# RetNet recurrence and SwiGLU block on one core: the half-head loads cut by token half, and the plan in another order

## The chip, the core and the metric

The kernel runs on one core of a Trainium2 chip. A core has a matrix engine (TensorE, PE in the profile, with its weight loads as PEld), a vector engine (VectorE, DVE), an activation engine (ScalarE, ACT), a general engine (GpSimd, POOL) and SyncE (SP), which here only waits and issues DMAs. Sixteen DMA engines carry the transfers. The metric is the device time of one execution in microseconds; runs of one kernel are given by their median.

## The reference

Two blocks follow one another. The first is a retention layer over q, k, v of shape (batch 4, heads 8, tokens 768, width 64):

```python
state = gamma[None, :, None, None] * state + np.einsum('bhd,bhe->bhde', k[:, :, t], v[:, :, t])
y[:, :, t] = scale * np.einsum('bhd,bhde->bhe', q[:, :, t], state)
```

with one decay gamma per head and scale 1/8. Its output, as 3072 tokens of 512 columns, is x for the second:

```python
g = x @ w_gate                      # 512 -> 1536
silu = g * (1.0 / (1.0 + np.exp(-g)))
val = x @ w_val
return (silu * val @ w_out).astype(np.float32)    # 1536 -> 512
```

## The kernel before, in words

**Segments.** The 3072 tokens are four batches of six chunks of 128 tokens. A segment is three chunks of each of two batches, 768 tokens; there are four segments, 0 to 3. Each has an up stage (gate and value products, SiLU, product of both into `hT`) and a down stage (`hT` times `w_out`). The retention of segment s+1 runs during the end of the up stage and in the down stage of segment s, between its matmuls.

**Words.** Matmuls run on float32r operands; each float32 operand is split into three words (lines 993 to 1010: a first word on ScalarE, a second on VectorE, a third on POOL or VectorE), and a product of K = 128 is three matmuls. The list `ELSE` names the steps that go to the other of two engines than usual: for third words VectorE in place of POOL.

**Segment 0** converts and splits all weights and keeps them in HBM: 12 up units `wup` (896 KB each) and 12 down units, split, `wdnt` (768 KB each). From segment 1 on, units come back by `load_unit` (`L`, line 1063) and `w_load` (`W`, line 1139). The up products of segments 1 to 3 use a seven-product scheme (`product`, line 1091): step `p f.n` is 6 matmuls of 128x384. A down step `D f.tok` (line 1160) is 3 matmuls of 128x512.

**Retention of segments 1 to 3.** A segment has three pairs p of chunks, one chunk from each batch. For a pair there are five loads `l`, issued by `load_pair`, n = 5p + w: w = 0 and 1 are k and q turned (head width on the partitions, line 789, 512 KB each in one DMA); w = 2, 3 and 4 are v, k and a second copy of q (line 793, 512 KB each in four DMAs of 128 KB, from `v_n`, `k_n`, `q_t`). These last three, the half-head loads, land as follows: of chunk c, partition 64 g + t and column 512 c + 256 z + n hold row 64 z + t, column 256 g + n of the source. So the partitions' lower and upper half hold the two halves of the 512 columns (g), and the two halves of the 128 rows (z; for v and k a row is a token) lie beside one another. The buffers (`homes`) are shared between pairs, so a load waits until what was in its home has been read.

The steps of a pair: `sc` (scores, line 798 by `scores_of`), `dec` (mask and decay), `q` (second q times decay, line 824 by 414, VectorE), `k` (k times decay, line 831, ScalarE), then `A` and `B` (`mix2`: scores times v, old state times q, and the growth of the state by k and v), `was`, `new`, `mv` (state), `y` (bank to `chunk_x`, line 1025), `sum` and `x` (the words of the next up stage's operand).

**Order.** All steps stand in one string, `PLAN`, 2345 names long; `run` calls them in that order, and each call appends its instructions to its engine's queue. Every engine works through its own queue in order; waits between engines are put in by the framework from what each instruction reads and writes. So the place of a name in `PLAN` sets its place in each queue that it touches. For SyncE that holds for `l`, `L`, `W`, `Z` (stores of split weights), `U` (raw weights) and `o` (stores of output tiles, line 1197): a DMA that waits for a buffer holds up all that stand behind it in the string.

Of the kernel before, what the change touches and what calls it, by code (L numbers as in the profile page):

```python
# [70 lines left out]
    G5:0 j4:0 n6:1 a8 G5:1 n6:3 U14:3 n5:5 W5:1 c7 i5:0 c14 i5:1
    Z13 U9:1 T5:1 j5:1 a14 U15:0 C7 W5:0 n7:0 T5:2 k5 n6:2 G6:0
    n6:4 n6:5 T6:0 T6:1 Z5 G6:1 g4 i6:0 n7:3 n7:1 n7:2 G7:0 T6:2
    j5:0 n7:4 W6:1 i6:1 n7:5 b14 b8 S14 C14 Z6 1/l1 R0 a9
    W6:0 S8 c8 C8 n8:0 n8:1 n8:2 b9 i7:0 h2 G7:1 j6:0 W7:0
    j6:1 S9 T7:0 n8:3 c15 c9 W7:1 Z14 a15 U10:2 U11:1 T7:1 C9
    n8:4 i7:1 j7:1 n8:5 b15 S15 T8:0 T7:2 U16:3 n9:0 G8:0 i8:0 G8:1
    n9:3 W8:1 T8:1 j7:0 n9:1 n9:2 T8:2 g5 a10 b10 S10 G9:0 k4
    i8:1 c10 Z7 a11 t4 C15 n9:4 C10 n9:5 W8:0 j8:1 T9:0 c16
    n10:0 b11 T9:1 Z15 G9:1 n10:3 a16 h1 n10:1 j8:0 n10:2 t5 b16  # L80
    1/l3 1/l0 S11 W9:1 W9:0 n10:4 S16 n10:5 i9:1 G10:1 c11 T10:0 C16
    C11 j9:1 i9:0 n11:0 1/cv0 Z8 U17:2 n11:1 j9:0 1/sc0 1/cv2 Z16 G10:0
    i10:1 1/cv3 0/h0.0 n11:2 1/l4 1/dec0.0 n11:3 1/k0.2 0/h0.1 W10:1 n11:4 n11:5 1/l7
    1/k0.0 i10:0 W10:0 1/l2 1/cv1 1/cm T11:0 1/dec0.1 1/q0.0 T11:1 T11:2 Z11 G11:0
    G11:1 a17 b17 0/h1.0 1/k0.1 1/k0.3 0/W0 0/W1 j10:1 S17 c17 C17 0/h0.2
    1/q0.1 1/was0.01 0/h1.1 j10:0 W11:0 i11:0 i11:1 1/l5 1/l6 0/d0.0 0/d0.1 j11:0 0/h1.2
    Z17 0/h2.0 0/h4.0 0/d1.0 1/was0.00 0/d0.2 W11:1 0/W2 0/d1.1 j11:1 T10:1 0/Z0 1/A0
    0/D0.0 0/d1.2 0/h2.1 0/D0.1 0/D0.2 1/sc1 1/l8 1/new0.0 0/h2.2 0/Z1 1/y0.00 0/d2.0 0/d2.1
    1/mv0.0 1/dec1.1 1/dec1.0 1/was0.11 0/D0.3 0/D1.0 0/D0.4 0/D0.5 0/h3.0 1/l9 0/d2.2 0/Z2 1/k1.3
    T9:2 T10:2 0/h4.1 0/D1.2 0/D1.3 0/D1.5 0/D1.1 0/h4.2 1/was0.10 1/y0.01 0/D1.4 1/k1.2 1/q1.0  # L90
    0/h5.0 0/W3 0/d3.0 0/d3.1 1/k1.1 0/h3.1 1/q1.1 1/B0 0/D2.0 0/D2.1 0/D2.2 Z10 Z9
    0/W4 1/begin 1/new0.1 0/d3.2 0/h5.1 0/h3.2 1/y0.10 1/y0.11 1/k1.0 1/mv0.1 0/D2.5 1/A1 0/D3.0
    1/x0.1.0 1/was1.00 1/x0.1.2 1/sum0.0 1/sum0.1 1/l10 0/Z3 0/D2.3 0/D2.4 0/W5 0/D3.4 0/D3.5 0/D3.1
    0/D3.2 0/d4.0 0/d4.1 1/was1.01 1/sum0.3 1/sum0.2 0/h6.0 1/l11 1/x0.2.0 1/x0.1.1 1/x0.0.0 1/x0.2.2 1/x0.2.1
    1/new1.0 1/l12 1/was1.10 1/y1.01 1/y1.00 0/d4.2 0/D4.0 0/h5.2 0/Z4 1/was1.11 1/x0.0.1 0/h6.1 0/d5.0
    0/h6.2 0/D3.3 0/D4.1 0/D4.3 0/W6 1/mv1.0 0/d5.1 1/B1 0/D4.5 0/D4.2 1/y1.11 0/d5.2 1/x0.0.2
    1/l13 0/D5.1 0/d6.0 0/d6.1 0/Z5 1/new1.1 1/y1.10 0/D4.4 0/h7.0 0/h8.0 1/sum1.0 0/D5.3 0/D5.0
    0/d6.2 0/D5.4 0/D5.5 0/D5.2 0/W7 0/h7.1 1/L0 1/k2.3 1/x1.1.0 1/mv1.1 1/k2.1 1/k2.0 0/h8.1
    0/h8.2 0/h7.2 0/Z6 0/W8 1/sc2 1/l14 0/d7.0 0/d7.1 1/x1.1.2 1/dec2.0 1/dec2.1 1/x1.2.0 0/h9.0
    1/was2.00 1/was2.01 0/D6.2 0/D6.5 0/D6.4 0/D6.3 0/D6.0 0/D6.1 1/L1 1/sum1.1 0/d7.2 0/W9 0/Z7  # L100
    1/sum1.3 1/x1.2.2 1/sum1.2 0/D7.5 1/x1.1.1 0/h9.1 0/d8.0 0/h10.0 0/d8.1 1/k2.2 0/D7.3 0/D7.0 0/D7.1
    0/D7.2 0/D7.4 1/x1.0.0 1/q2.0 1/q2.1 0/d8.2 0/Z8 0/h9.2 1/A2 0/D8.0 0/d9.0 0/h11.0 0/D8.1
    1/y2.00 0/d9.1 0/D8.3 0/D8.4 0/D8.5 0/D8.2 1/x1.0.2 1/x1.2.1 1/y2.01 0/d9.2 0/D9.0 0/h10.1 0/h10.2
    1/x1.0.1 0/W10 0/d10.0 0/d10.1 0/W11 1/w0.0.0 0/Z9 1/new2.0 1/mv2.0 0/D9.3 0/D9.2 1/B2 0/D9.1
    0/h11.1 0/d10.2 0/Z10 1/w0.0.1 1/L2 1/y2.10 1/y2.11 0/d11.0 0/D10.0 1/x2.2.0 0/D10.2 0/D10.1 1/sum2.0
    1/sum2.2 1/sum2.1 0/D9.5 0/D9.4 1/w0.1.0 1/w0.2.0 1/x2.1.0 0/d11.1 0/d11.2 0/D10.3 1/sum2.3 0/Z11 0/h11.2
    1/x2.0.0 0/D10.4 1/w0.0.2 1/x2.1.2 1/x2.1.1 0/D11.3 0/D11.1 0/D11.2 0/D11.0 0/e2 0/e0 1/x2.0.2 0/D10.5
    1/w1.2.0 0/D11.4 1/x2.0.1 1/w1.0.0 0/D11.5 1/w1.1.0 0/o2 1/x2.2.2 1/p0.0 1/w0.1.1 1/w0.1.2 1/p0.1 1/x2.2.1
    0/e1 1/u0.0 1/p0.2 1/w2.1.0 1/w1.0.1 1/p0.3 1/u0.3 1/u0.1 1/w1.0.2 1/p0.4 1/w2.2.0 0/o0 0/e4
    0/o4 0/o1 1/w0.2.1 1/L3 1/w0.2.2 1/p1.1 1/p1.0 1/w1.1.1 1/u0.4 1/u0.2 1/p0.5 1/w2.0.0 1/u0.5  # L110
    1/u0.6 1/p0.6 1/u1.0 1/p1.2 1/w2.0.1 1/w1.1.2 1/u0.8 1/w1.2.1 1/p1.3 1/w2.0.2 1/u1.3 1/p1.4 1/L4
    1/u1.1 1/u0.9 1/p2.0 1/w3.2.0 1/w3.1.0 1/w2.1.1 1/u1.4 1/w1.2.2 1/w3.1.1 1/u1.5 1/w2.1.2 1/u2.0 1/p1.5
    1/w3.0.0 1/u1.6 1/p2.1 1/u2.1 1/w2.2.1 1/p1.6 1/u1.8 1/w4.2.0 1/w3.1.2 1/u1.9 1/p2.2 1/L5 1/w3.0.1
    1/p2.3 1/u2.3 1/p2.4 1/w2.2.2 1/u2.4 0/e3 1/w3.2.1 1/w3.0.2 1/p2.5 1/u1.2 0/o3 1/u2.5 1/p2.6
# [12 lines left out]
    1/p8.1 1/u8.1 1/w10.2.0 1/w9.2.2 1/w9.1.2 2/l0 1/u7.9 1/w10.2.1 1/p8.2 1/u8.3 1/p8.3 1/p8.4 1/u8.4
    1/p8.5 1/w10.1.0 1/w10.0.0 1/u8.5 1/w9.0.2 1/u8.2 1/w10.1.1 2/l1 1/w10.1.2 1/p8.6 1/w10.0.1 1/u8.6 1/w10.0.2
    1/u7.7 1/p9.0 1/u8.8 1/w11.2.0 1/u9.0 1/p9.1 1/u9.1 1/p9.2 1/p9.3 1/u9.3 1/p9.4 1/u9.4 1/p9.5
    1/w11.1.0 2/sc0 2/l4 2/l2 1/u8.7 1/w11.0.0 1/u9.2 1/u9.5 1/p9.6 1/u8.9 1/w11.2.1 1/w11.1.1 1/w11.1.2  # L130
    1/u9.6 1/p10.0 1/u9.8 1/p10.1 1/w11.0.1 2/l5 1/W0 1/u10.0 1/p10.2 1/u10.3 2/dec0.1 1/u9.9 2/l6
    1/p10.3 1/u10.1 1/u10.2 2/dec0.0 1/p10.4 2/q0.0 1/u9.7 1/u10.4 1/p10.5 1/h0.0 1/u10.6 1/h1.0 1/u10.5
    1/h0.1 1/w11.0.2 1/w10.2.2 1/p11.0 1/p11.1 1/u11.0 1/p11.2 1/u11.1 1/u11.2 1/u10.7 1/h1.1 1/h0.2 1/p10.6
    1/u11.3 1/p11.3 1/u10.8 1/W1 1/u10.9 1/p11.4 1/h1.2 1/u11.4 1/p11.5 1/h2.0 1/h4.0 1/u11.5 2/l8
    2/q0.1 1/w11.2.2 1/p11.6 1/u11.8 2/begin 1/u11.6 1/u11.7 1/D0.0 1/W2 1/h2.1 1/D0.3 1/D0.1 1/u11.9
    2/k1.1 1/h4.1 2/A0 2/new0.0 2/sc1 2/l9 2/l7 2/y0.00 1/h4.2 1/h2.2 1/D0.2 2/mv0.0 2/dec1.0
    2/dec1.1 1/D1.2 1/D1.0 1/D0.4 1/D0.5 1/D1.5 1/W3 2/l10 1/D1.4 2/k1.0 2/was0.11 1/h3.0 2/was0.10
    2/q1.0 2/k1.3 2/y0.01 1/D1.3 1/D1.1 1/W4 1/h5.0 2/k1.2 1/h3.1 1/h5.1 2/q1.1 1/D2.0 1/D2.1
    2/B0 1/h5.2 1/D2.3 1/D2.5 1/D2.2 2/new0.1 2/y0.11 2/mv0.1 1/D2.4 1/W5 2/y0.10 2/l12 2/was1.01
# [244 lines left out]
def tile_retnet_swiglu(  # L384
# [394 lines left out]
    def two_of(t):  # L779
        return t.rearrange("p (z n) -> p z n", z=2)  # L780
# [551 lines left out]
```

## Time and profile before

| | |
|---|---|
| median of 3 runs | 668.71 us (659.56, 668.71, 670.72) |
| profiled execution | 666.25 us, its span 664.1 us |
| mean granted TensorE clock | 0.987 |
| busy: PE / PEld / DVE / ACT / POOL | 642.2 / 589.1 / 495.2 / 391.7 / 183.8 us |
| DMA | 144.59 MB, mean 218 GB/s over the span |
| DMA issues of line 793 (half-head loads) | 108, 128 KB each |
| DMA issues of line 1139 (split down weights) | 39 |

The span runs from the first to the last instruction of the profiled execution. The page divides it into 40 equal slices of 16.6 us and gives for each the busy share of an engine in tenths, the granted clock of TensorE, the mean busy share of the 16 DMA engines, and what they moved. In time: segment 0's attention and up stage run to 138 us, its down stage to 208; the up stages of segments 1 to 3 start at 208, 366 and 524, and their down stages at 303, 454 and 608. The half-head loads of segment 1 are issued from 110 to 180 us, those of segment 2 at 228 and from 287 to 340, those of segment 3 at 374 and from 438 to 493.

A line of a view of one source line gives engine, operation, tiles, count, and the duration of one in ns (least, median, greatest); for an instruction of SyncE that is the time of the issue, not of the transfer. "DMA to landing" is from issue to the last of its landing marks. A line of the view of waits gives who waited for whom, the total in us, how many times and the longest.

### The profile page before, as it was taken

The numbers are of one execution on the slowest core, as the hardware profiler recorded it, in microseconds if no ns is written. First come the engines' busy times: TensorE is split into PE (matmuls) and PEld (weight loads), VectorE is DVE, ScalarE is ACT, GpSimd is POOL, SyncE is SP. The second block draws the span as 40 slices with busy tenths as digits, with TensorE's granted clock in tenths as the row PEclk, the third lists the DMA queues.
The fourth block names the chain that finished last, engine by engine and source line by source line (L and its number), as shares of the span: only waits on it lengthen the run. The fifth ranks groups of instructions, "written<-read, shape, count | busy, mean of one in ns | idle before, by whom it ended". The sixth has DMA issues, their size and how long they took to land.

```text
span 664.1 us, 14143 instructions
## 1 busy us (share of the span) xinstructions
PE 642.2 (97%) x5587; PEld 589.1 (89%) x5587; DVE 495.2 (75%) x760; ACT 391.7 (59%) x815; POOL 183.8 (28%) x122
## 2 busy tenths in 40 slices
PE   8999999998989989999999999999889999999997
PEld 7999989886869979998878999999678899999886
DVE  3988687867989947787689778787678788777541
ACT  3778788966655656556667665546474465554221
POOL 1442545420112745520000514520000524452000
PEclk9999999997999979999999999999899999999999
DMA  9899987897986651456884724446976643403564
GB/s 314 275 353 302 373 275 256 301 321 305 319 282 217 226 157 57 154 192 210 281 308 170 255 77 167 143 147 199 287 230 229 212 153 128 167 0 100 199 220 148
DMA packets 60850, 144.59 MB, mean 218 GB/s; under 512 B 5872, under 2 KB 33008, under 8 KB 60784
## 3 DMA queue, kind: packets, MB, share of 16 engines
q1 hardware_dynamic: 60208, 142.90, 63.3%
q8 instruction: 44, 0.72, 0.4%
q10 hardware_dynamic: 576, 0.79, 0.4%
q14 instruction: 22, 0.18, 0.1%
HBM read 113.78 MB, written 29.88 MB: 216 GB/s over the span
## 4 chain that ended last, share of the span: by engine, by line
PE 58%; DMA 4%; ACT 1%; SPq 0%; issue 0%; DVE 0%; ACTq 0%
PE bank L1091 35%; PE bank L1160 19%; DMA oitem<-wdnt 3%; PE bank L798 3%; DMA loads<-in_k_n_dram 0%; SPq L793 0%; ACT loads L831 0%; ACT states L889 0%; ACT gitem L994 0%; DVE chunk_x L1183 0%; ACT tmp L1106 0%; ACT bank L1107 0%; ACT chunk_x L1185 0%; ACT bank L1110 0%; ACT xb L1003 0%
## 5 line engine op out<-in xcount | busy, mean ns | idle before, releaser
L1160 PE MATMUL bank<-oitem,gitem 128*128 128x512 f32 x867 | 209.0, 398 | 6.2 <-DMA oitem<-wdnt 4.6
L1160 PEld LDWEIGHTS bank<-oitem,gitem 128*128 128x128 f32 x867 | 163.0, 191 | 43.0 <-DMA oitem<-wdnt 2.4
L1091 PE MATMUL bank<-xa,gitem 128*128 128x384 f32 x864 | 159.9, 339 | 3.3 <-ACT tmp L1106 3.3
L1091 PEld LDWEIGHTS bank<-xa,gitem 128*128 128x128 f32 x864 | 152.9, 191 | 4.0 <-ACT tmp L1106 3.6
L1000 POOL TENSOR_TENSOR gitem<-gitem 128x768 fp32r<-128x768 f32 x48 | 96.3, 2016 | 175.1 <-DVE gitem L997 154.0
L1000 POOL TENSOR_TENSOR oitem<-oitem 128x256 fp32r<-128x256 f32 (+1 forms) x51 | 56.1, 1103 | 167.8 <-DVE oitem L997 149.8
L922 PE MATMUL bank<-xa,oitem 128*128 128x384 f32 x480 | 85.3, 336 | 2.1 <-DVE hT L459 1.1
L922 PEld LDWEIGHTS bank<-xa,oitem 128*128 128x128 f32 x480 | 82.9, 188 | 3.6 <-DVE hT L459 1.8
L997 DVE SCALAR_TENSOR_TENSOR gitem<-gitem,loads 128x768 fp32r<-128x768 f32 x72 | 75.9, 1069 | 11.4 <-ACT gitem L994 11.3
L1091 PE MATMUL bank<-xb,gitem 128*128 128x384 f32 x432 | 81.8, 335 | 0.0
L994 ACT ACTIVATE gitem<-loads 128x768 fp32r<-128x768 f32 x72 | 58.8, 841 | 34.8 <-PE bank L1091 26.2
L1091 PEld LDWEIGHTS bank<-xb,gitem 128*128 128x128 f32 x432 | 75.8, 188 | 0.2
L414 DVE SCALAR_TENSOR_TENSOR gitem<-gitem 128x768 fp32r<-128x768 f32 x72 | 71.2, 994 | 1.9
L997 DVE SCALAR_TENSOR_TENSOR gitem<-gitem,hT 128x768 fp32r<-128x768 f32 x48 | 46.0, 962 | 23.3 <-ACT gitem L994 23.2
L994 ACT ACTIVATE gitem<-hT 128x768 fp32r<-128x768 f32 x48 | 39.9, 840 | 36.8 <-PE bank L1160 29.6
L1091 PE MATMUL bank<-xb,oitem 128*128 128x384 f32 x216 | 43.8, 337 | 0.0
L1108 DVE TENSOR_TENSOR hT<-bank,tmp 128x384 f32<-128x384 f32 x36 | 20.0, 555 | 30.6 <-PE bank L1091 29.9
L1107 ACT COPY tmp<-bank 128x384 f32<-128x384 f32 x36 | 17.2, 477 | 36.0 <-PE bank L1091 20.1
L1091 PEld LDWEIGHTS bank<-xb,oitem 128*128 128x128 f32 x216 | 38.0, 188 | 0.2
L889 ACT ACTIVATE states<-states,local 128x64 f32<-128x64 f32 x120 | 31.5, 335 | 1.5 <-DVE states L897 1.5
L1025 ACT COPY chunk_x<-bank 128x256 f32<-128x256 f32 x36 | 12.4, 367 | 30.4 <-DVE states L897 16.1
L1108 ACT COPY tmp<-bank 128x384 f32<-128x384 f32 x36 | 17.3, 480 | 14.1 <-PE bank L1091 14.0
(125 smaller groups left out, 786.2 us busy)
## 6 DMA issues: line engine op xcount, KB each, us to landing
loads<-wup SPq DMA_DIRECT2D x36, 896.0 KB, 5.0
oitem<-wdnt SPq DMA_DIRECT2D x33, 768.0 KB, 5.2
wdnt<-oitem SPq DMA_DIRECT2D x12, 768.0 KB, 5.3
wup<-first SPq DMA_DIRECT2D x9, 896.0 KB, 6.4
rawp<-in_w_gate_dram SPq DMA_DIRECT2D x12, 512.0 KB, 7.4
rawp<-in_w_val_dram SPq DMA_DIRECT2D x12, 512.0 KB, 6.5
rawp<-in_w_out_dram SPq DMA_DIRECT2D x12, 512.0 KB, 7.1
out_dram<-chunk_x SPq DMA_DIRECT2D x21, 256.0 KB, 2.3
```

What stands on the lines that cost most here:

```text
L414: stt(o, x, 1.0, y, op0=mul, op1=op)
L798: nc.tensor.matmul(o, a, b, start=start, stop=True, skip_group_check=True)
L889: act(states[:, z, g, n], states[:, 1 - z, g, n], AF.Copy, scale=lg[:, ds(NP * g + n, 1)])
L922: nc.tensor.matmul(o, w[:, a, ts(b, P)], X0[:, a, i, NC - 1 - b], start=a == b == 0, stop=a == 2 and b == NC - 1, skip_group_check=True)
L994: act(o[0], x, AF.Copy, scale=CUT / FAR)
L997: stt(o[1], f32(o[0]), -FAR, x, op0=mul, op1=add)
L1000: op(o[2], f32(o[0]), f32(o[1]), op=add)
L1025: copy(cx[:, ds(2 * r, 2), :, half[z]], y)
L1091: nc.tensor.matmul(o, w[:, a, k], x[:, a, KH - 1 - k], start=start and a == k == 0, stop=a == 2 and k == KH - 1, skip_group_check=True)
L1107: lambda: act(gate, c11, AF.Silu, scale=ONE), lambda: copy(u2, x),
L1108: lambda: copy(p5, wb), lambda: tt(h1, x, p5, op=add),
L1160: nc.tensor.matmul(banks[tok][:, cols], hs[f][:, a, ds(i * TH + u * P, P)], wo[f][:, a, cols], start=f == a == 0, stop=f == NF - 1 and a = ...
```

## The change

Two things are changed; all else is as it was.

**The half-head loads.** The four DMAs of a load were made per chunk c and per half g of the partitions: each wrote 64 partitions, two pieces of 256 columns in each, from all 128 rows and one half of the columns. Now they are made per chunk c and per half z of the rows: each writes all 128 partitions, one piece of 256 columns in each, from 64 rows and both halves of the columns. Every element lands where it did. A DMA still moves 128 pieces of 1 KB, and there are as many DMAs.

```diff
         for c in range(2):
-            for g in range(2):
+            for z in range(2):
                 nc.sync.dma_start(
-                    out=two_of(t[half[g], ts(c, 512)]),
-                    in_=src[c, :, ts(g, 256)].rearrange("(z t) n -> t z n", z=2))
+                    out=t[:, ds(512 * c + 256 * z, 256)],
+                    in_=src[c, half[z]].rearrange("t (g n) -> g t n", g=2))
```

**The order.** The first 150 names of `PLAN` stay; the 2195 behind them are the same names in another order. Half of all names move by at most 5 places, one in four by 11 or more, one in a hundred by more than 24. The farthest: the stores `0/o5`, `0/o4` and `2/o4` go 114, 221 and 247 places back, `2/l7` 63 forward, `3/l7` 38 back. Some rows that hold the loads:

```diff
-    1/l3 1/l0 S11 W9:1 W9:0 n10:4 S16 n10:5 i9:1 G10:1 c11 T10:0 C16
+    1/cv3 h1 i9:0 1/l3 j9:1 n11:0 n11:1 j9:0 n11:2 1/l2 U17:2 Z8 1/l4
...
-    1/w11.1.0 2/sc0 2/l4 2/l2 1/u8.7 1/w11.0.0 1/u9.2 1/u9.5 1/p9.6 1/u8.9 1/w11.2.1 1/w11.1.1 1/w11.1.2
+    1/w11.1.0 1/u8.7 1/u9.2 1/u9.5 1/p9.6 1/u9.8 1/w11.0.0 2/sc0 2/l4 2/l2 1/u8.9 1/p10.0 1/w11.2.1
+    1/w11.1.1 1/w11.1.2 1/p10.1 1/u9.6 1/u9.7 1/u9.9 1/w11.0.1 2/dec0.1 2/l7 2/l5 1/W0 1/u10.0 1/u10.1
...
-    2/k1.1 1/h4.1 2/A0 2/new0.0 2/sc1 2/l9 2/l7 2/y0.00 1/h4.2 1/h2.2 1/D0.2 2/mv0.0 2/dec1.0
```

The order of SyncE's steps around the loads of segment 2, before and after:

```
before  2/sc0 l4 l2 l5 W0 l6 W1 l8 W2 A0 sc1 l9 l7 W3 l10 W4 B0 W5 l12 l11 A1 W6 B1 l13 W7 sc2 W8 l14 A2 W9
after   2/sc0 l4 l2 l7 l5 W0 l6 W1 l8 W2 sc1 A0 l9 W3 l10 W4 B0 l12 W5 l11 A1 W6 B1 l13 W7 W8 sc2 l14 A2 W9
```

The list `ELSE` loses 16 names and gains 18, third words of weights nearly all:

```diff
-    "0/d1.1", "0/d11.1", "0/d4.1", "0/d5.1", "0/d8.1", "0/d9.1", "0/e3",
+    "0/d0.1", "0/d1.1", "0/d11.1", "0/d3.1", "0/d4.1", "0/d5.1", "0/d8.1",
...
```

More of the change, by code (lines that the diff above doesn't have):

```diff
@@ L71 @@
[L71 to L78, printed above, removed]
@@ L97 @@
[L97 to L102, printed above, removed]
@@ L229 @@
[L229 to L231 removed]
+    U4:3 c3 Z0 n2:1 v0:2 Z1 n2:3 y1:1 p1:2 U13:1 a4 n2:2 v1:2
+    U5:2 S12 C12 y0:2 C3 G2:1 u1:2 n2:4 n3:0 n3:1 n3:2 n2:5 b4
+    Z12 G2:0 n3:3 h0 S4 y1:2 c4 i2:0 W2:0 G3:0 W2:1 n3:4 C4
+    T3:0 U6:3 a5 n4:0 i2:1 n3:5 j2:0 W3:0 G3:1 c13 T2:0 T3:1 T3:2
@@ new lines @@
+    n8:2 G8:0 W7:0 c15 S9 c9 C9 n8:3 Z14 1/l1 U10:2 U11:1 U16:3
+    T7:1 j7:0 n8:4 i7:1 a15 n8:5 i8:0 b15 T7:2 W7:1 j7:1 T8:0 S15
+    T8:1 g5 n9:0 T8:2 n9:1 G8:1 W8:1 n9:2 n9:3 i8:1 a10 j8:1 W8:0
+    b10 S10 c10 j8:0 C10 n10:0 n10:1 G9:0 Z7 a11 b11 c16 C15
+    n9:4 T9:0 n9:5 t4 G9:1 1/l0 Z15 t5 W9:1 W9:0 n10:3 n10:4 n10:5
+    n10:2 T9:1 S11 a16 b16 S16 i9:1 G10:1 c11 T10:0 C16 C11 1/sc0
+    1/cv3 h1 i9:0 1/l3 j9:1 n11:0 n11:1 j9:0 n11:2 1/l2 U17:2 Z8 1/l4
+    i10:1 Z16 1/dec0.0 1/cv2 0/h0.0 1/cv0 G10:0 n11:3 n11:4 T11:0 T11:1 T11:2 Z11
@@ new lines @@
+    1/mv1.0 0/d5.0 0/d5.1 0/d5.2 1/x0.0.2 0/h6.2 0/D4.1 0/W6 1/B1 1/y1.11 1/l13 0/d6.0 1/was1.11
+    0/d6.1 0/Z5 1/new1.1 1/y1.10 0/D4.5 0/D4.2 1/sum1.0 0/D5.3 0/D4.4 0/h7.0 1/mv1.1 0/h8.0 0/D5.0
+    0/D5.4 0/d6.2 0/D5.2 0/D5.5 0/D5.1 0/D6.5 0/D6.4 1/sc2 0/W7 0/h7.1 1/L0 1/k2.3 1/x1.1.0
+    1/k2.0 1/k2.1 1/x1.2.0 0/h8.1 0/h7.2 1/x1.1.2 0/h8.2 0/Z6 0/W8 1/l14 0/d7.0 1/dec2.0 1/dec2.1
+    1/was2.00 0/h9.0 1/was2.01 0/d8.0 1/k2.2 0/D6.1 0/D6.2 0/D6.3 1/sum1.1 1/sum1.3 0/d7.1 0/d7.2 0/D6.0
+    0/D7.0 1/L1 0/W9 0/Z7 1/sum1.2 1/x1.2.2 0/D7.2 0/D7.1 0/h9.1 0/h10.0 0/d8.1 0/D7.3 0/D7.5
@@ new lines @@
+    2/x0.0.0 2/x0.0.2 1/h6.2 1/D4.0 1/D3.1 2/x0.0.1 2/y1.01 1/W6 1/D4.3 2/B1 2/y1.10 2/y1.11 2/x1.1.0
+    2/sum1.0 2/sum1.1 1/D4.5 1/D5.5 1/D5.2 1/D4.4 1/D4.1 1/D5.1 2/l13 2/sum1.2 2/was1.11 2/new1.1 2/mv1.1
+    2/L0 1/D5.3 1/D5.4 1/D5.0 1/W7 1/W8 1/D6.0 1/D6.3 2/sc2 1/D6.2 2/k2.3 2/was2.01 1/h7.0
+    1/h8.0 2/sum1.3 2/x1.1.2 2/x1.1.1 1/h7.1 1/h7.2 2/dec2.1 1/D6.1 2/l14 2/k2.1 2/k2.2 2/k2.0 2/dec2.0
+    1/h8.1 1/D6.5 1/D6.4 2/L1 1/h8.2 1/h9.0 2/x1.2.0 2/x1.2.1 2/q2.0 2/x1.2.2 2/q2.1 1/D7.1 1/D7.2
@@ new lines @@
+    2/u8.0 2/p8.2 2/u8.3 2/p8.3 2/u8.4 2/u7.7 2/u8.1 2/u8.2 2/p8.4 2/w10.2.1 2/u8.5 2/p8.5 2/u8.6
+    2/w10.1.0 2/w10.1.1 2/w10.1.2 3/l1 2/w9.2.2 2/p9.0 2/u9.0 2/p8.6 2/w11.2.0 2/u8.8 2/w11.2.1 2/w11.2.2 2/u8.9
+    2/p9.2 2/p9.1 2/u9.1 2/u9.3 2/p9.3 2/u9.4 2/w10.0.0 2/p9.4 2/p9.5 2/w11.1.0 2/w10.0.1 2/w10.0.2 2/w10.2.2
+    3/sc0 3/l4 2/u9.5 3/dec0.1 2/u9.2 2/p9.6 3/dec0.0 2/u9.6 2/u9.8 2/u9.9 2/u9.7 2/w11.0.0 2/w11.0.1
+    2/w11.0.2 3/l6 2/p10.0 2/p10.1 2/W0 3/l2 2/u8.7 2/u10.0 2/p10.2 2/u10.3 2/p10.3 2/w11.1.1 2/w11.1.2
@@ new lines @@
+    2/D4.3 2/D4.2 3/mv1.0 3/was1.11 3/was1.10 3/B1 3/l13 3/new1.1 3/y1.10 2/D4.4 2/D4.5 2/W7 2/h7.0
+    3/y1.11 2/h8.0 3/x1.2.0 3/x0.0.2 3/sum1.0 3/sum1.1 3/L0 2/D5.4 3/was2.01 3/k2.3 2/h7.1 3/x1.2.1 3/x1.2.2
+    3/sum1.3 2/D5.2 2/D5.5 2/D5.1 3/sc2 3/l14 3/k2.0 3/was2.00 3/mv1.1 3/k2.1 3/k2.2 2/h8.1 2/h7.2
+    2/h8.2 3/sum1.2 2/D6.5 3/dec2.1 3/dec2.0 2/D6.2 2/D5.3 2/D5.0 2/h9.0 2/h9.1 2/W8 2/D6.1 2/D7.1
+    2/D6.4 3/x1.1.0 3/L1 3/x1.0.0 3/x1.1.2 2/D6.0 2/D7.0 2/D6.3 2/D7.2 2/h10.0 3/q2.0 3/x1.1.1 3/q2.1
```

298 lines of the change are left out of this document (140 added, 158 removed).

## The prediction

> **What bounds the kernel now.** The page first: who is busy, and at what clock.
>
> ```profile
> PE 642.2 (97%) x5587; PEld 589.1 (89%) x5587; DVE 495.2 (75%) x760; ACT 391.7 (59%) x815; POOL 183.8 (28%) x122
> ...
> PEclk9999999997999979999999999999899999999999
> DMA  9899987897986651456884724446976643403564
> ...
> q1 hardware_dynamic: 60208, 142.90, 63.3%
> ```
>
> TensorE works 97% of 664.1 us, at full clock but for three short dips, so the matmuls set the time and an order of steps can win at most the 22 us in which TensorE rests and the dips. The last line is the one that the rest hangs on: of the 16 DMA engines' time 63.3% is taken, and in the first third of the span the row of tenths stands at 8 and 9.
>
> Next the waits of TensorE, and the views of the two lines that issue the attention loads and the down weights:
>
> ```profile
> PE bank L1160 <- DMA oitem<-wdnt: 4.6, 3, 2.0
> PE bank L1091 <- ACT tmp L1106: 3.3, 1, 3.3
> ```
>
> ```profile
> L793 SPq DMA_DIRECT2D loads<-in_q_t_dram x36: 595/600/1494, 120.5 to 492.5; - x36
> ...
> DMA to landing us min/median/max: 2.5/3.5/8.6
> ```
>
> ```profile
> L1139 SPq DMA_DIRECT2D oitem<-wdnt x39: 319/320/1467, 293.1 to 648.4; - x39
> ```
>
> The longest total wait is for a down weight, 4.6 us in three places. SyncE's one queue carries those weights and the 108 half-head loads of L793, each 600 ns to issue against 320 for a weight.
>
> Last, the three stretches in which the half-head loads run, by windows (length, busy time of each engine, clock, DMA share, GB/s):
>
> ```profile
> 110.00:185.00 75.00, 71.41 (x868) 61.23 (x867) 58.74 (x95) 54.62 (x135) 18.09 (x12) 0.95 0.89 300
> ...
> 287.00:345.00 58.00, 56.80 (x714) 48.85 (x711) 43.55 (x68) 36.79 (x95) 3.68 (x3) 1.00 0.77 258
> ...
> 438.00:500.00 62.00, 58.05 (x758) 49.90 (x751) 43.90 (x71) 37.57 (x94) 4.55 (x3) 0.97 0.75 230
> ```
>
> TensorE has no room there, and the DMA engines have little: 11%, 23% and 25%.
>
> **The loads, step by step.** Before, one issue moves 128 pieces of 1 KB: destination 64 partitions with two pieces each, source 64 rows with two pieces each; the outermost count is 64 on both sides. After, it moves the same 128 pieces to the same places, but the destination is 128 partitions with one piece each, and the source is written (g, t, n): two column halves outermost, 64 rows inside each. What decides is over how many DMA engines this is dealt. In the trace each of the 343 issues has 16 landing marks (5488 in all), so all 16 engines took part each time; but every one has 64 or 128 outermost on both sides. So the trace bounds the new form from both ends only: 16 engines, if the 128 destination rows are dealt out, two, if the two outermost source pieces are. No transfer in the trace shows a cut along an inner dimension, and the nearest rows differ in just this point; I take two.
>
> The Trainium skill, page "DMA: Bandwidth & Descriptors", section "Why a DMA increments its semaphore by 16 and not by 1", says that the number of engines is the largest up to 16 that divides the outermost dimension (over one) of both access patterns, and that on the queue of SyncE they are the lowest-numbered ones. The 16 marks of each issue agree with it for 64 and 128; no run here shows it for two. By it the sum is the one below; by another row of that page ("Rules for kernel authors": one 128-partition transfer rather than two of disjoint partition halves) it would be the first rival.
>
> Price of a piece: 63.3% x 16 x 664.1 us / 60208 packets is 0.112 us for a mean 2373 bytes, so 48 ns for 1 KB. With 16 engines an issue is 8 pieces on each, 0.39 us, and a load (four issues) 1.54 us. With two it is 64 pieces on each, 3.08 us, and a load 12.34 us, and if the two are the same each time, all loads queue there. Down weights, up weights and k/q loads are cut over all 16, so each has a share on those two, in order of issue behind the half-head loads: a weight is there only when its slowest share is. That puts the price on the path: first the down steps (L1160), then the attention products, wait.
>
> Now each stretch, as work of one of the two engines (share x length, less the loads at the old price, plus the loads at the new, less the stretch):
> - 110 to 185, 9 loads: 66.8 - 13.9 + 111.1 = 164.0, over by 89 us.
> - 287 to 345, 8 loads (the ninth, `2/l3`, went alone at 228): 44.7 - 12.3 + 98.7 = 131.1, over by 73.
> - 438 to 500, 8 loads: 46.5 - 12.3 + 98.7 = 132.9, over by 71.
>
> That is 233 us. It is high, since the share holds packets stretched by the crowd: the trace's 1 KB packets have a median of 46 ns and the 6 and 7 KB ones 234 and 272, and at these the same sums give 75 + 63 + 57 = 195. With two engines at work and 14 mostly waiting the crowd is gone, so I take a value nearer to the low end, 205. The two loads left out of the stretches (228 and 374) fall into up stages at shares of 0.41 and 0.46 and cost nothing; in a busy stretch each would cost its 10.8.
>
> Can the new order hide it? It moves the loads little: `2/l7` comes before the first down weight and `3/l7` behind the second; `1/l3` comes behind `1/sc0`. The queue order of SyncE is else nearly the old one: W0 stands behind two or three loads, and `l13` still waits for B1, `l14` for the second-pair scores. Nothing starts an up stage earlier.
>
> **The rest of the change.** SyncE's issue: from 600 ns to between 320 (a weight's one-piece rows) and 600 (the same split source), 0 to 30 us of 664 on a queue with gaps; beside two engines that are late it is worth nothing, alone it is in the first rival. The new order moves steps by 5 places in the median and by 24 at the 99th percentile; instructions, durations and matmuls are the same. Stores `0/o4`, `0/o5` and `2/o4` go 100 to 250 places later; a store is 256 KB, 0.7 us of each DMA engine, and frees SyncE from a wait (L1197 on L1191 was 22.0 us in six); nobody asks for their buffer in the up stage. The list ELSE loses 16 steps and gains 18: mostly third words of weights that go from POOL (1.10 or 2.02 us) to VectorE (0.53 to 1.0) and back, behind TensorE's queue on engines at 28% and 75%. Order and list together are worth between +22 (all rest of TensorE gone) and a loss of the same size; I take 0, as the old waits are short and spread, and in the stretches they lie inside the long ones. Half clock after a wait: the dips read 0.95 over 75 us, so some 4 us; between two late loads it is hidden, after the last load of a stretch it costs up to about 4 us each.
>
> Sum: the profiled execution took 666.25 us (span 664.1 and 2.1 around it), and 666 + 205 gives 871; I say 870. The runs shown have a median of 668.71, 0.4% above it, and reach from 659.56 to 670.72: 2% is about what a measurement of this kernel can tell from no change.
>
> **The rivals.**
> 1. All 16 engines carry the new form (the 128 destination rows are dealt out). Then a load stays at 1.54 us, and the gain is the shorter issue where a weight stands behind L793: three weight waits of 4.6 us, half of a dip of 3.4 us, and the 1.2 us before a state decay at 339: 7.5 us at most, 659 us. The order can add or take some 10 to either side: 650 to 677, not slower. For it: the destination is the shape of the weight loads. Against: the source is not. It decides as soon as the landing of a load stays at 3 to 4 us.
> 2. Two engines, but others at each issue. Then there is no shared queue, and each load lands 3.08 - 0.39 = 2.7 us later. Nine groups of attention products (three in each of three stages) wait that long at most: 24 us, so 666 to 690, and 678 where half of it is hidden. Against: nothing in the trace shows a choice that changes.
> 3. Two engines with their queue, but the quiet stretches before take part of it: 185 to 228 has a share of 0.65, 228 to 287 of 0.41, 345 to 438 of 0.46, so 15, 35 and 50 us are free. Were loads issued that early, 100 us would go: 770. Against: the buffers are freed by the stage itself. It is the low end of the forecast's range, as 666 + 233 + 31 = 930 is the high one (three times 4 us of half clock, and 19 us in which the two engines stand still because SyncE waits for a buffer).
>
> **Chances.** Forecast (two fixed engines) 0.84, rival 1 0.11, rival 2 0.05. Its own range of 770 to 940 holds nearly all of the first, so 0.81 altogether, and the range stops there. Slower by over 2% (above 682): 0.84 and 0.02 of rival 2, 0.86. Within 2%: 0.09 of rival 1 and 0.03 of rival 2, 0.12. Faster: 0.02.
>
> **What would show it.** The view of L793: a median of over 8 us from issue to landing, where it was 3.5; under 4 if rival 1 holds, about 6 with rival 2. TensorE's waits: L1160 behind oitem<-wdnt and L798 behind loads, tens of us each, in place of 4.6. The row of DMA tenths: about 4 in the three stretches (66.8 us of work in some 155), which grow to some 155, 125 and 120 us, while the up stages keep their length. The landing marks: two late ones, 14 at once, in each L793 issue. The prediction is wrong if TensorE's busy share stays above 95%, and too high if packets of 1 KB go faster than 46 ns on a queue of their own.

## The result, and the profile after

| | before | after |
|---|---|---|
| median (runs) | 667.75 us (5: 659.21 to 670.72) | 879.24 us (5: 875.26 to 881.18) |
| ratio | | 1.324, 95% interval 1.312 to 1.335 |
| profiled span | 664.1 us | 877.6 us |
| mean granted TensorE clock | 0.987 | 0.883 |
| issues of L793: SyncE's time in them | 71 us | 257 us |

The kernel is 32% slower. The page of after, in the parts that the prediction read of before (busy time; tenths of the clock and of the DMA engines in 40 slices, now of 21.9 us each; the queue's packets, MB and share of 16 engines):

```profile
PE 686.5 (78%) x5587; PEld 620.0 (71%) x5587; DVE 503.5 (57%) x768; ACT 390.8 (45%) x812; POOL 179.0 (20%) x117
...
PEclk9999995777769989976788898998677879999999
DMA  9899824445546443215445452523234446441454
...
q1 hardware_dynamic: 58696, 142.90, 48.1%
```

The same matmuls and the same bytes; TensorE goes from 97% of the span to 78%, and the DMA engines from 63.3% to 48.1%. The queue has 1512 packets fewer than before, 14 for each of the 108 issues of L793: the landing marks of 14 engines, which no longer carry a piece.

TensorE's waits in after (who waited for whom, us in total, times, longest):

```profile
PE bank L1160 <- DMA oitem<-wdnt: 57.2, 8, 22.9
PE bank L798 <- ACT chunk_x L1025: 28.2, 5, 18.4
PE bank L798 <- DVE loads L414: 23.5, 6, 6.5
PE bank L922 <- DVE hT L459: 23.1, 1, 23.1
PE bank L798 <- DMA loads<-in_k_t_dram: 15.4, 2, 9.9
PE bank L1091 <- ACT tmp L1106: 14.2, 2, 8.0
```

The first was 4.6 us before; the next three were 1.9, 0.6 and 1.1. The waits behind L414 hang on half-head loads, and so do the 23.1 us behind L459, ahead of which VectorE had stood 23.6 us for a second q. The longest one behind L1025 came after ScalarE had waited 11.7 us for a raw down weight. In the view of L793 (issues with least, median and greatest ns of an issue; then who waited for what they bring) the loads are what VectorE and ScalarE wait for.

```profile
L793 SPq DMA_DIRECT2D loads<-in_q_t_dram x36: 512/2536/5384, 130.2 to 700.7; - x36
L793 SPq DMA_DIRECT2D loads<-in_v_n_dram x24: 534/2632/4721, 115.0 to 620.2; - x24
...
  DVE loads L414: 90.1, 13
  ACT tmp L831: 72.0, 6
  ACT loads L831: 32.7, 6
```

The median of all 108 issues is 2.6 us where it was 0.6. A piece of SyncE's timeline of after (start, length, engine, line) shows two loads, eight issues, in 21.68 us, with a k load and a down weight behind them:

```profile
363.57 5.43 SPq L793 DMA_DIRECT2D loads<-in_q_t_dram  x4
369.04 21.68 SPq L793 DMA_DIRECT2D loads<-in_v_n_dram  x8
390.82 2.46 SPq L789 DMA_DIRECT2D loads<-in_k_t_dram  x1
393.38 0.99 SPq L1139 DMA_DIRECT2D oitem<-wdnt  x1
```

And windows of after: that piece first, then the three stretches with half-head loads (length, busy time of PE, PEld, DVE, ACT, POOL, clock, DMA share, GB/s):

```profile
363.50:390.00 26.50, 15.47 (x96) 14.44 (x87) 15.21 (x23) 7.97 (x15) 4.52 (x4) 0.90 0.13 45
...
109.00:262.00 153.00, 87.34 (x976) 72.97 (x973) 67.96 (x104) 60.20 (x142) 17.78 (x11) 0.77 0.46 161
...
363.00:479.00 116.00, 70.84 (x794) 58.04 (x784) 41.76 (x67) 36.57 (x95) 5.02 (x4) 0.79 0.37 123
...
589.00:707.00 118.00, 73.22 (x841) 61.09 (x833) 46.69 (x76) 37.42 (x95) 2.53 (x2) 0.78 0.36 115
```

A DMA share of 0.13 is two engines of sixteen, and while they work alone 45 GB/s move. The stretches grew from 75, 58 and 62 us to 153, 116 and 118; from the start of the last up stage to the end it is 140 us in both kernels. The trace's DMA records name no engine, but they show how many packets are under way; counted for each tenth of a us, with two packets read as two engines at work:

```
stretch of after   length   two packets on way    none on way
109 to 262          153           81.9 us             1.2 us
363 to 479          116           73.8                1.3
589 to 707          118           72.0                4.9
```

So for 228 us two engines worked and fourteen stood by. That they are the same two each time is seen in transfers that are cut over all 16: their marks come in two lots, fourteen early and two some 4 us late. Of the 68 such transfers that were issued in the three stretches, 64 have two marks over 1 us behind the fourteen. Three examples (ns after the issue; the last row is a half-head load's issue, whose fourteen idle marks come at once and whose two real ones late).

```
390.82 L789   fourteen 5648 to 6028    two 9899, 10521
393.38 L1139  fourteen 5479 to 5811    two 9219, 9836
369.04 L793   (14 at once) 2958        two 10210, 10756
```

Between 369.5 and 388 us 871 half-head pieces of 1 KB went, which is one in 42.5 ns on either engine. An issue is 64 of them, 2.72 us, which is about what SyncE's issues take: with some four issues (10.5 us of work) outstanding, SyncE stood in the next one until the engines had done one more.

### The profile page after: what moved, and what is told of

Its sections match the earlier page's. It is cut to its first block, busy times and chain, and to the rows that moved or that the text cites. A ratio compares the mean times of both kernels' runs of the same rounds, so it can differ in the third digit from the quotient of the medians.

```text
span 877.6 us, 14120 instructions
## 1 busy us (share of the span) xinstructions
PE 686.5 (78%) x5587; PEld 620.0 (71%) x5587; DVE 503.5 (57%) x768; ACT 390.8 (45%) x812; POOL 179.0 (20%) x117
## 3 DMA queue, kind: packets, MB, share of 16 engines
q1 hardware_dynamic: 58696, 142.90, 48.1%
## 5 line engine op out<-in xcount | busy, mean ns | idle before, releaser
L1160 PE MATMUL bank<-oitem,gitem 128*128 128x512 f32 x867 | 232.8, 427 | 69.6 <-DMA oitem<-wdnt 57.2
L1160 PEld LDWEIGHTS bank<-oitem,gitem 128*128 128x128 f32 x867 | 176.7, 208 | 115.9 <-DMA oitem<-wdnt 54.5
L1091 PE MATMUL bank<-xa,gitem 128*128 128x384 f32 x864 | 162.4, 343 | 15.6 <-ACT tmp L1106 14.2
L1091 PEld LDWEIGHTS bank<-xa,gitem 128*128 128x128 f32 x864 | 155.7, 194 | 16.9 <-ACT tmp L1106 15.0
L922 PE MATMUL bank<-xa,oitem 128*128 128x384 f32 x480 | 88.0, 343 | 23.9 <-DVE hT L459 23.1
L1000 POOL TENSOR_TENSOR oitem<-oitem 128x512 fp32r<-128x512 f32 (+1 forms) x47 | 55.3, 1180 | 236.6 <-DVE oitem L997 210.4
L922 PEld LDWEIGHTS bank<-xa,oitem 128*128 128x128 f32 x480 | 85.6, 193 | 25.4 <-DVE hT L459 23.4
L994 ACT ACTIVATE gitem<-loads 128x768 fp32r<-128x768 f32 x72 | 59.1, 842 | 27.0 <-PE bank L1091 21.9
L414 DVE SCALAR_TENSOR_TENSOR gitem<-gitem 128x768 fp32r<-128x768 f32 x72 | 69.7, 974 | 1.4 <-DVE gitem L997 0.5
L414 DVE SCALAR_TENSOR_TENSOR loads<-loads,tab 128x512 f32<-128x512 f32 x18 | 12.4, 689 | 90.1 <-DMA loads<-in_q_t_dram 83.9
L831 ACT ACTIVATE tmp<-tmp,local 128x128 f32<-128x128 f32 x24 | 8.5, 394 | 72.0 <-DMA tmp<-in_k_n_dram 72.0
L1025 ACT COPY chunk_x<-bank 128x256 f32<-128x256 f32 x36 | 12.2, 366 | 57.5 <-PE bank L798 35.1
L1107 ACT COPY tmp<-bank 128x384 f32<-128x384 f32 x36 | 17.2, 478 | 40.5 <-PE bank L1091 19.6
```

The lines of the kernel that those rows point to most:

```text
L414: stt(o, x, 1.0, y, op0=mul, op1=op)
L922: nc.tensor.matmul(o, w[:, a, ts(b, P)], X0[:, a, i, NC - 1 - b], start=a == b == 0, stop=a == 2 and b == NC - 1, skip_group_check=True)
L994: act(o[0], x, AF.Copy, scale=CUT / FAR)
L1000: op(o[2], f32(o[0]), f32(o[1]), op=add)
L1025: copy(cx[:, ds(2 * r, 2), :, half[z]], y)
L1091: nc.tensor.matmul(o, w[:, a, k], x[:, a, KH - 1 - k], start=start and a == k == 0, stop=a == 2 and k == KH - 1, skip_group_check=True)
```

## The experiments

Two figures serve all of them. The **extra work** of a load in the form after is 64 x 4 x 42.5 ns = 10.88 us on each of two engines less the 1.54 us that it was, 9.34 us. The **spare time** of an engine in the three stretches before is 8 + 13 + 16 = 37 us (11%, 23% and 25%), which the prediction subtracted. It belongs to the kernel that one compares with: in the one with 128 source rows below, whose stretches are 71.5, 57 and 58.5 us at DMA shares of 0.93, 0.82 and 0.78, it is 28 us.

**Loads alone, order alone.** Theory: the loads are the whole loss. Rival: the order has a part in it, as it puts down weights behind two or three loads. The first kernel has the order before and the loads after, the second the loads before and the order after (edits against after).

```diff
 loads alone: PLAN and ELSE of before
-    U4:3 c3 Z0 n2:1 v0:2 Z1 n2:3 y1:1 p1:2 U13:1 a4 n2:2 v1:2
+    U4:3 c3 Z0 n2:1 v0:2 Z1 n2:3 U13:1 a4 p1:2 y1:1 n2:2 S12
...
 order alone: the loads of before
-                    out=t[:, ds(512 * c + 256 * z, 256)],
-                    in_=src[c, half[z]].rearrange("t (g n) -> g t n", g=2))
+                    out=two_of(t[half[g], ts(c, 512)]),
+                    in_=src[c, :, ts(g, 256)].rearrange("(z t) n -> t z n", z=2))
```

> The old order with the new half-head loads. If the two outermost pieces of the source put each load on two engines (theory), the whole loss is here: 860 to 900 us, each issue of line 793 with 3 landing marks in place of 16, 2.6 us from issue to issue where they follow one another. If the new order were the cause (rival), this would stay at 660 to 680 us.

> The new order with the old half-head loads. Theory: the order is worth little, 650 to 680 us, 16 marks for every issue. Rival (the order brings the loss): 850 us or more.

Measured beside 662.98 us of before: loads alone 880.04 us, ratio 1.330 (1.324 to 1.336), order alone 656.16 us, ratio 0.990 (0.986 to 0.995). The loads are the whole loss; the order alone is a gain of 1.0%, invisible behind them (879 and 880 us with either order). TensorE's waits for transfers in the kernel with the order alone:

```profile
PE bank L798 <- DMA loads<-in_k_t_dram: 3.2, 1, 3.2
PE bank L1160 <- DMA oitem<-wdnt: 1.8, 4, 0.6
```

The 4.6 us for down weights of before are 1.8.

**One piece per row, eight issues.** If the source's outermost count of two is the cause, issues of 64 rows with one piece each are carried by all engines again. The price is twice as many issues.

```diff
-                nc.sync.dma_start(
-                    out=t[:, ds(512 * c + 256 * z, 256)],
-                    in_=src[c, half[z]].rearrange("t (g n) -> g t n", g=2))
+                for g in range(2):
+                    nc.sync.dma_start(
+                        out=t[half[g], ds(512 * c + 256 * z, 256)],
+                        in_=src[c, half[z], ts(g, 256)])
```

> The new order and the cut by token half, but each DMA taken apart into its two column halves: 64 partitions, 64 source rows, one piece of 1 KB each, eight DMAs of 64 KB per load in place of four of 128 KB. The outermost count is 64 on both sides. Theory: 16 engines again, back to 655 to 690 us, in spite of twice as many issues (at 0.57 us, as the 64-row loads of line 761 show, 4.6 us of SyncE per load where the old form takes 2.4). Rival (the cut by token half, or its 1 KB reads at a pitch of 2 KB from 64 rows, is what is slow): 850 us or more.

Measured: 693.32 us (690.83 to 696.52), ratio 1.048 (1.042 to 1.054). With the form go 186 of the 211 us, and the time is 3 us above the upper end of what was expected. The view of its L794 (L793 of after) and the chain (shares by engine):

```profile
L794 SPq DMA_DIRECT2D loads<-in_q_t_dram x72: 465/547/1702, 122.2 to 526.3; - x72
```

```profile
PE 72%; DMA 15%; DVE 5%; SPq 4%; issue 3%; ACT 1%; POOL 0%; ACTq 0%; DVEq 0%; POOLq 0%
```

Half the pieces make an issue hardly shorter (547 ns here, 587 in the median of all 216, against 600), so a load takes SyncE 4.9 us in place of 2.6 (132.9 and 70.6 us for 27 loads). The kernel takes 37 us more than the order alone, whose chain has 1% of SyncE and 7% of DMA where this one has 4% and 15%: with 16 engines at work twice the issues are a cost by themselves. How much of it is SyncE's time and how much the smaller transfers, no run separates.

**The source's count alone, 128 and 4.** This is the test of the cause: destinations, pieces, number of issues and order as after. Three further inputs hold the same numbers in another arrangement, so that the source of an issue is 128 rows (first kernel), or four blocks of 32 rows with an unused row behind each (second).

```diff
-        src = (k_t, q_t, v_n, k_n, q_t)[w][one : two + 1 : two - one]
+        src = (k_t, q_t, v_h, k_h, q_h)[w][one : two + 1 : two - one]
...
-                    in_=src[c, half[z]].rearrange("t (g n) -> g t n", g=2))
+                    in_=src[c, z])                  # v_h[chunk, z, 128, 256]
+                    in_=src[c, z, :, 0:32])         # second: v_h[chunk, z, 4, 33, 256]
```

> The order after, four issues per half-head load with the same destinations (128 partitions, 1 KB each) and the same 128 pieces; only the source differs: three further inputs hold v, k and q with the 128 pieces of an issue in 128 rows one behind the other, so that the source's outermost count is 128 and not 2. Nothing is left out. If the source's count of 2 is the whole cause: the time of the new order alone, 656 us (650 to 668), 16 landing marks per issue, 3 to 5 us from issue to landing. Rival: the cause is the new destination or that an issue now takes a half of the rows in place of a half of the columns: 850 to 880 us as after. If the issue is shorter for one-piece rows than the 600 ns of before: up to 5 us below 656.

> As the kernel with 128 source rows, but the inputs hold the 128 pieces of an issue in four blocks of 32 rows with an unused row behind each block, so that the source's outermost count is 4. Nothing is left out. If the number of engines is that count: 4 engines, 32 pieces on each, some 1.4 us per issue and 5.4 per load (after: 10.6); landing marks 2 to 4 later than the rest. The sum of the shared queue then gives 26 + 18 + 15 = 60 us over 656: 716; in proportion to the load's price over 1.5 us, 3.9/9.1 of 224 us: 751. Rival: engines are dealt out in another way and 2 was a special case: 656 (all 16) or 880 (two).

Measured beside 664.0 us of before: 128 rows 647.31 us (646.13 to 648.27), ratio 0.976 (0.971 to 0.982); four blocks 735.81 us (732.02 to 737.43), ratio 1.109 (1.102 to 1.116). The queue's packets, in order: 128 rows, four blocks.

```profile
q1 hardware_dynamic: 60208, 142.90, 64.8%
```

```profile
q1 hardware_dynamic: 58912, 142.90, 58.4%
```

The first is the count of before to the packet; the second has 1296 fewer, 12 for each of 108 issues: 16, 4 and, in after, 2 engines, as the source's outermost count. The destination's 128 rows and the cut by rows play no part. From the kernel with 128 rows, its loads and two of TensorE's waits:

```profile
L796 SPq DMA_DIRECT2D loads<-in_q_h_dram x36: 327/383/2926, 120.0 to 478.4; - x36
...
DMA to landing us min/median/max: 2.0/4.2/6.7
```

```profile
PE bank L1162 <- DMA oitem<-wdnt: 0.8, 1, 0.8
...
PE bank L800 <- DVE loads L417: 0.4, 1, 0.4
```

This is 9 us below the order alone. An issue takes 0.38 to 0.43 us in place of 0.60, 53 us of SyncE's time against 72 with the order alone, and half of that difference arrives. (The pieces of an issue also lie one behind another in HBM here, which no run separates.) Against it, and not against before, the form after costs 879.2 - 647.3 = 232 us.

Four engines were to cost 60 us over 656 by the sum of the queue, with the spare time used, and 95 in proportion to the price of a load; over the 647 of 128 rows they cost 88.5. TensorE again waits for weights, then for loads:

```profile
PE bank L1162 <- DMA oitem<-wdnt: 21.1, 7, 10.0
PE bank L800 <- DVE loads L417: 11.5, 4, 4.4
PE bank L800 <- ACT chunk_x L1027: 11.4, 3, 8.6
```

**Every third load in the form after.** The order before; only the second q loads (w = 4) have the new form. The theory then was the prediction's: what does not exceed the spare time is free.

```diff
+                if w == 4:
+                    nc.sync.dma_start(
+                        out=t[:, ds(512 * c + 256 * i, 256)],
+                        in_=src[c, half[i]].rearrange("t (g n) -> g t n", g=2))
+                else:
                     nc.sync.dma_start(
```

> The old order; of the three half-head loads of a pair only the second q is in the new form. The theory of a shared queue on two engines takes the sum over the stretches: with 10.4 us per new load and 1.5 per old one the stretches are over by 9 to 19, 7 to 14 and 2 to 11 us, so 685 to 712 us, less than a third of the loss, since the rest fits into the 11 to 25 percent that the engines had free. A rival in which each new load costs its own delay, queue or not, gives a third of the loss, 71 us: 737 us.

Measured: 738.86 us (734.83 to 739.72), ratio 1.115 (1.108 to 1.122): 76 us for a third of the loads. The rival's figure, in proportion to the loads, is right here, and the prediction's subtraction is not. Its waits:

```profile
PE bank L1165 <- DMA oitem<-wdnt: 22.7, 5, 10.9
PE bank L803 <- DVE loads L414: 22.4, 5, 6.5
```

About as much falls on weights behind the loads as on the second q itself, which L414 scales. That left two readings: the queue of the two engines can't use its spare time, or it is the late landing of the loads themselves that costs.

**The same work for nobody.** The kernel with 128 source rows, and behind each second q load its four issues once more in the form after, from HBM to a place in HBM that nothing reads.

```diff
+        if w == 4:
+            raw = q_t[one : two + 1 : two - one]
+            for c in range(2):
+                for z in range(2):
+                    nc.sync.dma_start(
+                        out=aside.pop().rearrange("(g t) n -> g t n", g=2),
+                        in_=raw[c, half[z]].rearrange("t (g n) -> g t n", g=2))
```

> As the kernel with 128 source rows (647 us), and behind each of the nine second-q loads its four issues again in the form after (source two column halves), from HBM to a place in HBM that nobody reads: 36 issues on two engines as in the kernel with every third load in the new form (75 us over its base), but no step waits for what they bring. Nothing of the computation is left out. They add 3 x 4 x 64 pieces x 42.5 ns = 32.6 us of each of the two engines to each stretch. If the cost is the queue of the two engines, less the spare share that they had: 24 + 19 + 17 = 60 us, 707. If the queue costs and its spare share can't be used: 3 x 32.6 = 98 us, 745. If the cost in that kernel was the late landing of the loads themselves, for which scores and state wait: 650 to 665.

Measured: 732.12 us (724.84 to 733.85), ratio 1.103 (1.096 to 1.110) and 85 us over its base: between the 60 and the 98 of the queue, far from the 650 to 665 of the late landing. The added issues, and the waits:

```profile
L803 SPq DMA_DIRECT2D as<-in_q_t_dram x36: 597/816/3074, 123.1 to 557.6; - x36
```

```profile
PE bank L1170 <- DMA oitem<-wdnt: 39.0, 6, 10.0
PE bank L808 <- ACT chunk_x L1035: 11.8, 1, 11.8
```

Transfers that nobody reads cost about as much as late loads: it is what stands behind them, the down weights first, that is late. But the 85 us are not the queue's alone. The 36 issues are added ones, they take SyncE 50 us, and SyncE is 6% of this kernel's chain (1% in its base). In the kernel with eight issues a load 108 more cost 37 us, which for 36 would be some 12 (an estimate); no run separates them. (They also write 4.7 MB to HBM, which the form after does not.)

**One issue of four.** The kernel with 128 source rows, but the first issue of each half-head load in the form after: 27 issues on two engines, evenly spread.

```diff
                     out=t[:, ds(512 * c + 256 * z, 256)],
+                    in_=raw[c, half[0]].rearrange("t (g n) -> g t n", g=2)
+                    if c == z == 0 else src[c, z])
```

> As the kernel with 128 source rows, but the first of the four issues of each half-head load keeps the form after (source two column halves of 64 rows): 27 issues on two engines in place of 108. Nothing is left out. Taking only every third load in the new form cost 71 us of 211 with 36 issues, which the sum of a shared queue did not give (28). Here the slow issues are spread evenly. Sum of the shared queue with the spare time of the two engines counted: 20 us, 676. In proportion to the number of slow issues: 27/108 of 224 us is 56, 712. If what counts is how late one load is (some 2.6 us here, 10.5 us there) beyond what each waiting step can stand: under 665.

Measured: 672.38 us (669.65 to 674.82), ratio 1.014 (1.008 to 1.020), 25 us over its base, where 20 were expected from the queue with its spare time used and 56 in proportion. Loads land in a median of 6.2 us against 4.2, and the longest wait of TensorE is 3.8:

```profile
DMA to landing us min/median/max: 4.7/6.2/7.5
```

```profile
PE bank L803 <- ACT chunk_x L1030: 4.6, 3, 3.8
...
PE bank L1165 <- DMA oitem<-wdnt: 3.1, 2, 2.6
```

With the measured price of a piece the five kernels stand side by side. The extra work is that of one engine that carries the form, over the loads inside the stretches (25 of 27; all nine second q loads). The spare time is that of the kernel compared with.

| kernel, compared with | extra work | less the spare time | measured |
|---|---|---|---|
| after (four issues a load, two engines), before | 25 x 9.34 = 234 | 197 | 211 |
| every third load, before | 9 x 9.34 = 84 | 47 | 76 |
| the same for nobody, 128 rows | 9 x 10.88 = 98 | 70 | 85 |
| four engines, 128 rows | 25 x (5.44 - 1.54) = 98 | 70 | 88 |
| one issue of four, 128 rows | 25 x (2.72 - 0.39) = 58 | 30 | 25 |

In the three kernels in the middle, where slow issues come in bunches of four and do not fill their engines, 8 of 37, 13 of 28 and 10 of 28 us of the spare time are used; where single slow issues stand between fast ones, all of it. A bunch holds what is behind it for 5 to 11 us, and when TensorE waits that long nothing more is asked of the engines that could fill their spare time. That last sentence is read from the table and the waits; no run shows it by itself. In after the two engines are full: by the prediction's sum with 10.88 us a load, one of them has 158 - 39 + 272 = 391 us of work in the three stretches, which are 387 us long and move 52.5 MB where 51.7 went before. There the spare time is used up: the stretches grew by 192 us, and what goes beyond that lies outside them.

**GpSimd's queue.** The kernel after with the loads issued by GpSimd, to see whether SyncE's being held is a cost beside the engines'.

```diff
-                nc.sync.dma_start(
+                nc.gpsimd.dma_start(
```

> The kernel after with the half-head loads issued by GpSimd's queue in place of SyncE's, nothing else changed and nothing left out. SyncE spent 257 us in these issues, so that weights and other loads could not be issued meanwhile. If the same two engines carry them and what costs is their share of every weight: 840 to 890 us. If SyncE being held is a large part of the 211 us, the weights of the down stage come early and the loads alone are late: 700 to 800. If that queue deals an issue out over more engines whatever the source's form: 16 landing marks, 650 to 690.

Measured: 751.36 us (746.2 to 754.05), ratio 1.135 (1.130 to 1.141). It doesn't answer the question, for two things changed at once. The queue made other transfers of them, and GpSimd, which makes third words of weights, now waits in order for buffers (the queue; the issues; in the same view what GpSimd waited for):

```profile
q0 software_dynamic: 29376, 14.55, 10.7%
```

```profile
L793 POOL DMA_DIRECT2D loads<-in_q_t_dram x36: 784/812/855, 127.9 to 563.6; - x36
...
  PE bank L798: 84.1, 12
```

The records of that queue hold 16 marks for each issue and pieces of 4 KB, 32 an issue, and up to 14 of them are under way at once: they are no longer on two fixed engines. Still each load lands 9.4 us after its issue in the median (3.5 in before), and 84 us of GpSimd's waits stand ahead of its words. Whether SyncE's hold costs anything beside the two engines' own queue stays open; in after there is little room for it, since in the stretches there were 7.4 us of 387 with no packet under way.

**One issue per load.** The order after, and each half-head load as one DMA of 512 KB from inputs arranged so that a partition takes two pieces of 2 KB, 128 outermost on both sides.

```diff
-        src = (k_t, q_t, v_n, k_n, q_t)[w][one : two + 1 : two - one]
...
+        src = (k_t, q_t, v_h, k_h, q_h)[w][one : two + 1 : two - one]
+        nc.sync.dma_start(out=two_of(t), in_=src.rearrange("c r n -> r c n"))
```

> The order after, each half-head load as one DMA of 512 KB, from the same three further inputs laid out so that each partition takes two pieces of 2 KB (128 outermost on both sides). Nothing is left out. 81 issues fewer, some 0.45 us each, 36 us of SyncE's time; TensorE waits for loads and weights only some 5 us in the kernel with the new order alone (656 us), so at most 5 us are to be had: 650 to 657. If SyncE's issue time were on the path beyond these waits: under 648.

Measured: 644.94 us (643.69 to 648.02), ratio 0.974 (0.967 to 0.981). It is the fastest kernel here, faster than before and after, but not to be told from the four issues over 128 rows (647.31; 0.971 to 0.982). SyncE's time in these issues is 11 us rather than 53, and some 2 us came of it, which is within the noise. With the inputs as they are, the order alone (656.16 us) is the best.

## Why the prediction was right, by its own steps

The forecast of 870 us (770 to 940) met 879.24, and the mechanism that it was put on, two fixed DMA engines, is the one that the runs show. Its sum was less right than its total, and that the total came within about 1% is partly luck (point 4).

1. **Two engines carry the new form: right.** Packet counts, the share of 0.13 and the marks show it in after, and the kernels with 128 and with 4 outermost source pieces show that the source's count alone decides. The Trainium skill, page "DMA: Bandwidth & Descriptors", section "Why a DMA increments its semaphore by 16 and not by 1", states the rule of the largest number up to 16 that divides both outermost counts, and that the lowest-numbered engines are taken. The runs agree: 16, 4 and 2 engines for 128, 4 and 2, and the two late marks of 64 of 68 transfers over all 16 fit a fixed choice (which two, no mark tells). The row of the same page that prefers one transfer over 128 partitions to two over halves ("Rules for kernel authors") is no help with this source: 879 us against 668. With a source of 128 rows 128 partitions gain, 647 us against the 656 of the order alone.
2. **The price of a piece: too high.** It was taken as 46 to 48 ns per KB. 46 ns is how long the record of such a piece lasts in the median, in the crowd of before and alone in after; but records overlap (the DMA share of before is 1.05 from 138 to 150 us), and from piece to piece an engine takes 42.5. A load is 10.88 us, not 12.34. This was named as what would make the forecast too high. With 10.88 the prediction's three lines give 76, 61 and 59 us, 196 in place of 233.
3. **The spare time of the engines: rightly subtracted here, but not as a rule.** The stretches grew by 78, 58 and 56 us, 192 together, close to those 196, and the two engines were full in them (391 us of work in 387). In kernels that do not fill them the same subtraction fails: every third load cost 76 us and not 47. The prediction had no condition for that.
4. **The stretches' lengths, and what was put at nothing.** Foretold were some 155, 125 and 120 us, measured 153, 116 and 118. The other 22 us of the loss lie in the pieces between them (in the windows, 23, 79, 21, 72 and 24 us became 17, 84, 28, 82 and 30, and the first stretch begins 1 us earlier). The step that failed is the single loads in the up stages, which were to "cost nothing" at DMA shares of 0.41 and 0.46. With the order of before, where matmul can be set beside matmul, the kernel with the loads alone loses 5.6 and 11.0 us in the pieces from 208 to 287 and from 366 to 438; the one with every third load, whose single loads keep the old form, loses nothing there (-1.6 and 0.0). In after ScalarE stood 6.3 us for the first of these loads, just before one of the two waits behind L1106 that make up the 14.2 us above. So the forecast's 205 us were 13 above the growth of the stretches, and 22 us beside it were missing: two errors that nearly cancel.
5. **Order and list at 0, between +22 and -22:** the order alone is worth -7 us (1.0%), inside the bounds, and nothing behind the late engines. Two readings on the way were off, and nothing hangs on them: of the names behind the first 150 half move by at most 3 places and one in ten by 11 or more, fewer than stated, and the DMA tenths of before in the first third of the span are 6 to 9, not 8 and 9.
6. **SyncE's issue, 0 to 30 us shorter: wrong for this form.** It became 3.6 times as long, 257 us against 71, since SyncE stands in an issue once some four are outstanding. "Worth nothing beside two engines that are late" held all the same. Where the engines are not late, the shorter issue came out as estimated: 0.38 to 0.43 us, and 9 us of time.
7. **Half clock hidden between late loads: right in effect, far larger in size.** TensorE's busy time rose from 642.2 to 686.5 us for the same matmuls, with a clock of 0.77 to 0.79 in the stretches. The two engines worked on meanwhile, so the 44 us are no term of the sum.
8. **The rivals.** All 16 engines (chance 0.11): fell for this source, and was priced at 659 us for a form that the kernel with 128 source rows runs in 647, as order and issue are worth more than the 7.5 us given. Two others each time: fell, the late pair is fixed. Quiet stretches that take part (770): fell, the loads are still issued in the stretches (109 to 245, 363 to 472 and 589 to 701 us, all but two of them), and the pieces between grew by 22 us together.
9. **What was to show it.** Weights at L1160 (57.2 us) and loads at L798, DMA tenths around 4, longer stretches and TensorE at 78%: as told. By the marks an issue of L793 landed after 11.3 us in the median (over 8 was foretold). The up stages did not all keep their length: from first to last product 95, 90 and 89 us became 101, 108 and 89.

## What to carry to other kernels

Before a DMA is rewritten, look at the outermost count of both of its patterns as they are written: here a transpose in the source's view (two halves ahead of 64 rows) put 128 KB on two of sixteen engines, and everything cut over all sixteen then waited for the slowest two. Price such a queue by its extra work, and by the time from piece to piece rather than by how long a record lasts. Count on the spare time of a mean DMA share only when the engines are full anyway or the slow transfers are spread out: where they came in bunches, 8 to 13 us of 28 to 37 were used. A single slow load in a stage at a share of 0.4 was not free either. And count issues as well as bytes: halving the pieces of an issue hardly shortened it, and eight issues in place of four cost more than the gain of the better order.

## What was not expected of the hardware

- SyncE was held in an issue, 2.6 us in the median and up to 7.0, once some four issues of 64 pieces per engine (10.5 us of work) were outstanding; with transfers over 16 engines issues of as many pieces took 0.38 to 0.60 us in the median.
- An issue of 128 pieces took 0.60 us with 64 rows of two pieces, 0.51 us with two halves of 64 rows (the least in after), 0.38 to 0.43 us with 128 rows of one; 64 rows of one piece took 0.55 to 0.59 us. The number of pieces alone does not set it.
- A fifth of the loss in time (44 of 213 us) appears as busy time of TensorE, through the clock after waits, while the two DMA engines set the time: a rising busy time is no sign that an engine has become the bound.
